# SyncE's queue in the source's order, result stores on GpSimd's queue, first row blocks modulated by feature block (adaLN block on one Trainium2 core)

## The chip, the cores and the metric

The kernel runs on one core of a Trainium2 chip. A core has TensorE (PE in the profile: matrix products and transposes; its weight loads are listed as PEld), VectorE (DVE), ScalarE (ACT), GpSimd (POOL) and SyncE (SP). SyncE computes nothing: its queue issues DMA transfers between the memory outside (DRAM) and the core's on-chip memory. ScalarE's and GpSimd's queues can issue transfers too. Each engine works through its own instructions in their order; semaphores hold an instruction until what it needs is there. The metric is the device time of one execution in microseconds.

## The reference

One adaptive-layer-norm block over x of shape (1, 2048, 576), all in float32:

```python
mod = (_silu(c) @ w_mod).reshape(c.shape[0], 6, 1, -1)
sa, ca, ga, sb, cb, gb = (mod[:, n] for n in range(6))
h = _layernorm(x, axis=-1) * (1 + ca) + sa
x = x + ga * _A_ref(h, A_wqkv, A_wo)
h = _layernorm(x, axis=-1) * (1 + cb) + sb
x = x + gb * _B_ref(h, B_w1, B_w2, B_w3, B_w4)
```

`_A_ref` is attention with 32 heads of 18 features, causal, in a sliding window of 256 positions. `_B_ref` first mixes tokens (layer norm, product with w1, gelu, four quarters of the features shifted by +1, -1, +2 and -2 positions, product with w2, added to its input) and then channels (layer norm, product with w3 to 4608 features, gelu, product with w4, added).

## The kernel before, in words

The 2048 rows are 16 row blocks of 128. The 576 features are four feature blocks of 128 and a tail of 64. Products that need float32 precision are made from parts: an operand is rounded to the matrix format (the high part), the difference is kept as a second operand (the low part), and three products (high with high, high with low, low with high) are added in PSUM, the memory that TensorE writes to.

Three phases follow one another.

**Phase A** (`phase_a`, to about 712 us) makes the modulation, the projections and the attention. `consts` makes masks on GpSimd; `vones` sets the constant columns of the 16 V tiles on GpSimd; `cond` loads c and makes silu(c), which a transpose turns into a column per feature block. `mod_load` loads the ten pieces of the modulation matrix for sa and ca (tiles wmL), `mod_mm` multiplies them with silu(c) (L243), `mod_ev` evicts the result with four activations (L250) and `mod_tr` transposes it into columns (modT, L258). `ln(t)` loads a row block (L268), makes its statistics (L85 to L89: VectorE's batch-norm instructions, then two small GpSimd instructions for the reciprocal root), normalizes it (L277), transposes it (L286, L288), and then, with the modulation as per-partition scale and shift, evicts it by feature block (L292), rounds it to the high part (L295) and subtracts for the low part on GpSimd (L297). Four row blocks share a tile hT. `vraw` and `vload` load and split the weights of V, `qload` those of q and k (L332 and the two loads L77 and L78 of `load_dup`); `vproj` (L357) projects V for a row block, `qproj` (L371) q and k for four of them, which ScalarE stores to DRAM (qkh, qkl: L376).

The attention works in 32 units: c counts four groups of 8 heads, g four groups of 512 positions, hq the two halves of a head group. A unit has a buffer of four (tiles U), made by `ualloc` (two memsets on GpSimd, L385 and L386). `uload` (L400) brings its queries and keys from DRAM in twelve DMAs. `s2` makes scores (L426) for the row maxima (L433 on VectorE), turns them into a row (L447, evicted as ms by ScalarE, L449) and writes them into the unit's queries by two DMAs on SP (L451: "the maxima"). `s3` makes the transposed scores (L476, with the mask by L477), the exponentials on ScalarE (L483, tiles P), the product with V (L498), its eviction (L503), a transpose (L510), the division on VectorE (L516, tile o), and stores o for two units at once to DRAM on SP (od, L518).

Beside the attention, `modvec` makes the other four modulation vectors: loads on SP (L189), multiplications on GpSimd (L193 to L196), a product with ones, and a store on SP (modd, L205). `woload` loads Wo, scales it with ga on GpSimd (L558), rounds it on ScalarE (L559) and subtracts on GpSimd (L560). `s4` makes the output projection of a row block: loads of od and x (L657, L659), transposes, products (L677) with the addition to x (L678) and a store (xp, L680); statistics; `ln1` modulates (L99, L101) and stores (hbd, L691); statistics again; `ln2` normalizes (L780) and stores (xnd, L696). `load_w1` and `load_w2` load and split the weights of phase B through two raw buffers (L716 to L761); the last step of `load_w2` writes the low parts of a tail into place by DMAs on SP (L761). Row blocks 12 to 15 go through `s4` in phase B.

**Phase B** (`phase_b`, to about 900 us) mixes tokens; its first row blocks are loaded from xnd (L797). **Phase C** (to the end) is the channel mix: 18 groups of 256 hidden features, products L1012 and L1041.

What sets the order: `phase_a` gives every step a time (`ev`, a list of time and function), with one attention unit as the unit of time; T0 is the time of the first projection, `shift` that of the first unit. `play` runs the steps in order of time, which writes the instructions down in that order: the source's order. Under `manual_schedule` the named engines keep this order, TensorE and GpSimd before the change. All other queues, SP among them, get their order from a planner that estimates durations and moves an instruction forward when it thinks that it could go. In phases B and C every queue is planned so.

Of the kernel before, what the change touches and what calls it, by code (L numbers as in the profile page):

```python
# [50 lines left out]
class Kern:  # L51
# [75 lines left out]
    def phase_a(self):  # L127
# [11 lines left out]
        with ExitStack() as st:  # L139
# [9 lines left out]
            ones = wp.tile([P, P], F32, name="ones")  # L149
            units = []  # L150
# [15 lines left out]
            def cond():  # L166
# [6 lines left out]
                nc.scalar.activation(sr, cr, AF.Exp, scale=-1.0)  # L173
                nc.vector.tensor_scalar(sr, sr, 1.0, None, op0=ALU.add)
# [6 lines left out]
            def modvec(v):  # L181
                acc = []
                steps = []

                def chunk(k):
                    def f():
                        w = row(f"wm{v}_{k}")
                        kk = P if k < KC else TAIL
                        nc.sync.dma_start(w[:kk], self.w_mod[k * P:k * P + kk, v * D:(v + 1) * D])  # L189
                        if k == 0:  # L190
                            acc.append(w)
                        if k == 0:
                            nc.gpsimd.tensor_scalar(w, w, silu[:, 0:1], 0.0, op0=ALU.mult, op1=ALU.add)  # L193
                        else:
                            nc.gpsimd.tensor_scalar(w[:kk], w[:kk], silu[:kk, k:k + 1], 0.0, op0=ALU.mult, op1=ALU.add)
                            nc.gpsimd.tensor_tensor(out=acc[0][:kk], in0=acc[0][:kk], in1=w[:kk], op=ALU.add)  # L196
                    return f

                def spill():
# [5 lines left out]
                    nc.sync.dma_start(self.modd[v], acc[0][0:1, :])  # L205

                steps = [chunk(k) for k in range(KC + 1)]
                return steps + [spill]
# [20 lines left out]
            def mod_bc():  # L229
                fm["s"] = fm["x"][:, 4 * P:4 * P + 32 * (KC + 1)].rearrange("p (k n) -> p k n", n=32)  # L230
                nc.vector.memset(fm["x"][:, 256:320], 0.0)
                nc.vector.tensor_copy(fm["s"], silu.unsqueeze(2).to_broadcast([P, KC + 1, 32]))

            halves = (slice(0, 256), slice(256, D))
# [11 lines left out]
            def mod_ev():  # L246
                fm["r"] = fm["x"][:, 0:320]
                for q in range(4):
                    n = halves[q % 2].stop - halves[q % 2].start
                    nc.scalar.activation(fm["r"][32 * q:32 * q + 32, 0:n], fm["p"][32 * q:32 * q + 32, 0:n], AF.Copy, bias=float(q // 2))  # L250
# [49 lines left out]

            Wv, Wq, wbuf = {}, {}, []
# [22 lines left out]

            def qload(m):
                def f():
                    raw = pp.tile([P, KC + 1, P], F32, tag="wr", name=f"rwq{m}", bufs=2)
# [3 lines left out]
                    cols = slice(m * P, (m + 1) * P)  # L331
                    nc.sync.dma_start(raw[:, 0:KC, :], self.wqkv[0:KC * P, cols].rearrange("(k p) c -> p k c", p=P))  # L332
                    self.load_dup(raw[:, KC, :], self.wqkv[KC * P:, cols])
# [13 lines left out]
            def vproj(t, z):  # L347
                def f():
                    L = hT[t // 4]
                    ts = slice((t % 4) * P, (t % 4 + 1) * P)  # L350
                    pv = dense([P, 288], f"pv{t}_{z}")
                    pl = []
                    for k in range(KC):
                        pl += [(L[:, k, ts], Wv[z, k][:, 0, :]), (L[:, k, ts], Wv[z, k][:, 1, :]), (L[:, KC + k, ts], Wv[z, k][:, 0, :])]
                    pl += [(L[:, 2 * KC, ts], Wv[z, KC][:, 0, :]), (L[:, 2 * KC, ts], Wv[z, KC][:, 1, :])]
                    for n, (a, b) in enumerate(pl):
                        nc.tensor.matmul(pv, a, b, start=(n == 0), stop=(n == len(pl) - 1))  # L357
# [21 lines left out]
            def ualloc(n):  # L379
                def f():  # L380
# [3 lines left out]
                    k = u[:, 2048:].rearrange("p (j n) -> p j n", j=2)  # L384
                    nc.gpsimd.memset(q.bitcast(F32), 0.0)  # L385
                    nc.gpsimd.memset(k.bitcast(F32), 1.0)  # L386
# [68 lines left out]
            def s3(c, g, hq):  # L455
# [50 lines left out]
                def fin2():  # L506
# [9 lines left out]
                    nc.vector.tensor_tensor(out=o[:, :, hq * 72:hq * 72 + 72].rearrange("p t (h d) -> p t h d", d=DH), in0=pt[:, :, :, 0:DH], in1=rc.unsqueeze(3).to_broadcast([P, 4, 4, DH]), op=ALU.mult)  # L516
                    if hq == 1:
                        nc.sync.dma_start(self.od[g].rearrange("(t p) d -> p t d", p=P)[:, :, c * 144:(c + 1) * 144], o)  # L518
# [10 lines left out]
                return steps, n, fin1, fin2  # L529
# [3 lines left out]
            def woload():  # L533
                steps = []

# [11 lines left out]
                steps.append(begin)  # L547

                def one(k):
                    def f():  # L550
                        raw = row(f"wor{k}")
                        if k < KC:
                            nc.sync.dma_start(raw, self.wo[k * P:(k + 1) * P, :])
                            h, l = Wo["m"][:, k, :], Wo["m"][:, KC + k, :]
                        else:
                            self.load_dup(raw, self.wo[KC * P:, :])
                            h, l = Wo["h"], Wo["l"]
                        nc.gpsimd.tensor_tensor(out=raw, in0=raw, in1=Wo["ga"], op=ALU.mult)  # L558
                        nc.scalar.copy(h, raw)  # L559
                        nc.gpsimd.tensor_tensor(out=l, in0=raw, in1=h.bitcast(F32), op=ALU.subtract)  # L560
                    return f
                return steps + [one(k) for k in range(KC + 1)]
# [8 lines left out]
            def sub3(c, g, hq, tb):  # L571
                st, n, f1, f2 = s3(c, g, hq)
                e = max(t for t, _ in st) / n * self.ww
                return [(tb + self.ww * t / n, f) for t, f in st] + [(tb + e + self.l_f, f1), (tb + e + self.l_f + self.l_o, f2)]
# [4 lines left out]
            ev = [(T0 - 2.0, consts), (T0 - 1.95, cond), (T0 - 1.97, warm(0)), (T0 - 1.9, vones), (T0 - 1.9, mod_bc)]  # L579
            for k in range(KC + 1):  # L580
                ev += [(T0 - 1.9 + 0.1 * k, mod_load(k)), (T0 - 1.3 + 0.1 * k, mod_mm(k))]
            ev += [(T0 - 0.85, mod_ev), (T0 - 0.8, mod_tr)]
# [14 lines left out]
            for kind, a, b in jobs:  # L597
# [5 lines left out]
                if kind == "v":  # L603
                    ev.append((T, vproj(a, b)))
# [5 lines left out]
            for t in range(NT):  # L610
                g, i = divmod(t, 4)
                ld, stt, nm, tr = ln(t)
                te = first["h", g] - 0.05 - (0.15 if g == 0 else 0.25) * (3 - i)
                tl = max(te - 1.6, T0 - 1.94 + 0.001 * t if t < 2 else T0 - 1.34 + 0.05 * t)
                ev += [(tl, ld), (max(te - 0.6, tl + 0.1), stt), (max(te - 0.4, tl + 0.15), nm), (te, tr)]
            ev += [(T0 - 1.35, vraw(0)), (last["v", 0] - 0.5, vraw(1))]
            for k in range(KC + 1):
                ev += [(T0 - 0.75 + 0.02 * k, vload(0, k)), (last["v", 0] + 0.01 + 0.005 * k, vload(1, k))]
            for n, m in enumerate(order):
                t1 = first["q", m] - (0.45 if m in early else 0.75)  # L620
                ev.append((t1 if n < 3 else max(t1, last["q", order[n - 3]] + 0.01), qload(m)))
            for n in range(4):
                ev.append((self.t_end - (8.99 - 3 * n) * dq, ualloc(n)))
# [3 lines left out]
            for c in range(NCH):  # L627
                for g in range(NGA):
                    for hq in range(2):
                        tb = 2 * u + hq + shift  # L630
                        ev.append((tb - self.u_ld, uload(c, g, hq)))
# [7 lines left out]
            uw = 2 * (3 * NGA) + 0.6 + shift  # L639
            ev += spread(woload(), uw, uw + 1.5)  # L640
            for n, v in enumerate((2, 3, 4, 5)):
                mv = modvec(v)
                ev += spread(mv[:-1], shift + 8.0 + 2.5 * n, shift + 10.0 + 2.5 * n)
                ev.append((shift + 11.3 + 2.5 * n, mv[-1]))
            ev += spread(self.load_w1(), 2 * u - 2 + 1.9 + shift, 2 * u + 1.6 + shift)
            ev += spread(self.load_w2(), 2 * u + 1.6 + shift, 2 * u + 2.4 + shift)
            with self.tc.manual_schedule(engines={mybir.EngineType.PE, mybir.EngineType.Pool}):
                play(ev)

    def s4(self, g, i):  # L650
# [14 lines left out]
        def wo(hf):  # L665
            def f():
# [12 lines left out]
                if hf == 1:  # L679
                    nc.sync.dma_start(self.xp[t], x)  # L680
# [7 lines left out]
        def ln1():  # L688
            x = box["x"]
            self.modulate(x, x, *box["s"], self.cb, self.sb, self.m_s4)  # L690
            nc.sync.dma_start(self.hbd[t], x)  # L691
# [421 lines left out]
```

## Time and profile before

| | |
|---|---|
| median of 3 runs | 1824.18 us (lowest 1822.40, one run of 5885.22) |
| the profiled execution | 1823.32 us |
| its span, first to last instruction | 1821.2 us |
| TensorE busy | 1744.1 us |
| VectorE, ScalarE, GpSimd busy | 979.7, 605.8, 386.1 us |
| mean granted TensorE clock | 0.982 |
| moved by DMA | 156.88 MB, 136.09 of them issued by SP |

Times in the profile are in us from the span's start. A row of a timeline gives start, duration, engine, line, operation, output and inputs by name, form and count, and in brackets the idle time before it and what ended that time. In the lists of waits a row reads: engine, tile and line that waited, what it waited for, then the total in us, how often, and the longest. SPq is SP's queue of DMA issues. U is a unit's buffer, wmL the modulation weights, wor and Wom are Wo raw and split, xr is a row block in `s4`, xn one in phase B.

### The profile page before, as it was taken

The page shows a single profiled execution, that of the slowest core. Times are in us where ns is not written, and L with a number is a line of the kernel's source. Part 1 is how long each engine was busy: PE and PEld are TensorE (multiplying, and loading weights), DVE is VectorE, ACT ScalarE, POOL GpSimd, SP SyncE. Part 2 cuts the span into 40 slices and gives each one's busy share as a digit, 9 for nine tenths or more (in the row PEclk, how much of TensorE's full clock was granted, in tenths as well). Part 3 has the DMA queues.
Part 4 walks back from the last instruction along what each step waited for, and adds up shares of the span by engine and source line. Part 5 has one row for each costly group of instructions (what it writes and reads, how often), then busy time and mean ns, then how long its engine had stood idle before and what let it go on. Part 6 is the DMA issues. An engine that isn't in the chain of part 4 may idle for free.

```text
span 1821.2 us, 30288 instructions
## 1 busy us (share of the span) xinstructions
PE 1744.1 (96%) x11700; PEld 1503.8 (83%) x11700; DVE 979.7 (54%) x2670; ACT 605.8 (33%) x1292; POOL 386.1 (21%) x376
## 2 busy tenths in 40 slices
PE   7999889989988998999899999999999999999999
PEld 5898666666665776999899999999999999999998
DVE  5302377767766887787744444444444444444434
ACT  5722156556555444444321111211111121111111
POOL 4511220022002111111313332333322111111100
PEclk8999999999999999999999999999999999999999
DMA  6424433454334455642301111111101000000002
GB/s 206 128 95 146 172 108 95 116 130 117 104 110 136 159 182 177 227 133 71 103 28 54 40 54 35 48 54 54 41 29 35 22 20 28 28 28 28 1 1 104
DMA packets 97904, 156.88 MB, mean 86 GB/s; under 512 B 11226, under 2 KB 40670, under 8 KB 97762
## 3 DMA queue, kind: packets, MB, share of 16 engines
q1 hardware_dynamic: 87394, 136.09, 25.3%
q10 hardware_dynamic: 10368, 18.88, 2.8%
q8 instruction: 92, 1.51, 0.3%
q14 instruction: 50, 0.41, 0.1%
HBM read 107.06 MB, written 47.20 MB: 85 GB/s over the span
## 4 chain that ended last, share of the span: by engine, by line
PE 56%; DVE 2%; POOL 0%; DMA 0%; issue 0%; ACT 0%; SPq 0%; POOLq 0%; ACTq 0%; DVEq 0%
PE p L1041 25%; PE p L1012 21%; PE pg L853 2%; PE w L906 2%; PE p L1014 2%; PE p L1013 2%; DVE x L907 0%; PE po L677 0%; DVE xr L99 0%; DMA r<-in_B_w_dram 0%; DVE G L871 0%; POOL CW L996 0%; DVE xm L780 0%; DVE LNT L70 0%; DVE G L858 0%
## 5 line engine op out<-in xcount | busy, mean ns | idle before, releaser
L1041 PEld LDWEIGHTS p<-CW,Gc 128*128 128x128 f32 x3456 | 474.4, 188 | 16.2 <-DVE Gc L1023 3.7
L1041 PE MATMUL p<-CW,Gc 128*128 128x288 f32 x3456 | 482.8, 295 | 3.4 <-DVE Gc L1023 3.4
L1012 PE MATMUL p<-LNT,CW 128*128 128x512 f32 x1728 | 419.8, 391 | 0.0
L1012 PEld LDWEIGHTS p<-LNT,CW 128*128 128x128 f32 x1728 | 316.7, 188 | 58.9
L1020 ACT ACTIVATE gfc<-p 128x512 f32<-128x512 f32 x144 | 86.1, 598 | 735.5 <-PE p L1014 735.5
L433 DVE CUSTOM_DVE_ANT_0 sc<-sc,mask 128x384 f32<-128x384 f32 (+2 forms) x512 | 262.9, 552 | 119.8 <-PE sc L426 116.9
L1045 DVE TENSOR_TENSOR acc<-p,acc 128x288 f32<-128x288 f32 x340 | 152.9, 454 | 316.1 <-PE p L1041 312.7
L483 ACT ACTIVATE P<-X 128x384 f32<-128x384 f32 x480 | 223.9, 489 | 148.6 <-PE X L477 143.4
L426 PE MATMUL sc<-U 126*128 126x384 f32 (+2 forms) x512 | 205.5, 415 | 29.8 <-DMA U<-qkl 13.9
L476 PE MATMUL X<-U 128*128 128x384 f32 (+2 forms) x704 | 182.6, 317 | 8.2 <-ACT P L483 7.6
L476 PEld LDWEIGHTS X<-U 128*128 128x128 f32 x704 | 128.7, 194 | 37.9 <-issue 26.1
L1045 DVE TENSOR_TENSOR accw<-p,accw 128x288 f32<-128x288 f32 x204 | 89.8, 452 | 130.1 <-PE p L1041 128.4
L477 PE MATMUL X<-maskb,identb 128*128 128x256 bf16 x480 | 138.3, 288 | 0.0
L426 PEld LDWEIGHTS sc<-U 126*128 126x128 f32 x512 | 101.3, 203 | 42.7 <-DVE m L433 17.5
L1023 DVE TENSOR_TENSOR Gc<-gfc,Gc 128x512 fp32r<-128x512 f32 x144 | 129.0, 896 | 4.7
L371 PE MATMUL pq<-hT,Wq 128*128 128x512 f32 x504 | 122.1, 401 | 0.7 <-DVE m L433 0.7
L371 PEld LDWEIGHTS pq<-hT,Wq 128*128 128x128 f32 x504 | 95.2, 191 | 23.3 <-DVE m L433 1.1
L992 POOL TENSOR_TENSOR CW<-r,CW 128x1024 fp32r<-128x1024 f32 x17 | 41.3, 2427 | 280.6 <-DVE CW L990 280.6
L498 PE MATMUL av<-P,V 128*32 128x256 f32 (+2 forms) x1472 | 96.6, 391 | 0.7 <-ACT P L483 0.7
L1022 ACT CAST Gc<-gfc 128x512 fp32r<-128x512 f32 x144 | 89.5, 621 | 4.6
L996 POOL TENSOR_TENSOR CW<-r,CW 128x1152 fp32r<-128x1152 f32 x17 | 46.4, 2727 | 158.5 <-DVE CW L995 158.5
L477 PEld LDWEIGHTS <-identb 128*128 128x128 bf16 x480 | 46.7, 97 | 38.7 <-issue 22.8
(1075 smaller groups left out, 1967.2 us busy)
## 6 DMA issues: line engine op xcount, KB each, us to landing
U<-qkh SPq DMA_DIRECT2D x160, 72.0 KB
U<-qkh SPq DMA_DIRECT2D x96, 108.0 KB
r<-in_B_w_dram SPq DMA_DIRECT2D x18, 576.0 KB
qkh<-hl ACTq DMA_DIRECT2D x36, 256.0 KB
qkl<-hl ACTq DMA_DIRECT2D x36, 256.0 KB
r<-in_B_w_dram SPq DMA_DIRECT2D x18, 512.0 KB
U<-qkl SPq DMA_DIRECT2D x80, 72.0 KB
U<-qkl SPq DMA_DIRECT2D x48, 108.0 KB
```

The costliest lines, as they stand in the source:

```text
L371: nc.tensor.matmul(pq, a, b, start=(n == 0), stop=(n == len(pl) - 1))
L426: nc.tensor.matmul(sc[:, lo:], QZ[:KR, q, i * P:(i + 1) * P], KZ[:KR, j, i * P + lo:(i + 3) * P], start=True, stop=True)
L433: nc.vector.tensor_tensor_reduce(out=sc[:, lo:], in0=sc[:, lo:], in1=mask[:, lo:], scale=1.0, scalar=-3e38, op0=ALU.add, op1=ALU.max, accu ...
L476: nc.tensor.matmul(X[:, x0:x0 + nb, :].rearrange("p a b -> p (a b)"), KZ[:, j, kb * P:(kb + 1) * P], QZ[:, q, qb * P:(qb + nb) * P], start ...
L477: nc.tensor.matmul(X[:, 0::2, :], self.identb, mk, start=False, stop=True)
L483: nc.scalar.activation(Pb[b][:, q, :], Xb[b, q].rearrange("p a b -> p (a b)"), AF.Exp, scale=SCALE)
L498: nc.tensor.matmul(abox[0][32 * q:32 * q + 32, q0:q0 + w], V[4 * g + kb][:, hv:hv + 32], Pb[b][:, q, p0:p0 + w], start=(first and n == 0), ...
L1012: nc.tensor.matmul(pg, W3[:, ws, fs], L[:, xs, :], start=(i == 0), stop=False)
L1022: nc.scalar.copy(Gh, gf)
L1023: nc.vector.tensor_tensor(out=Gl, in0=gf, in1=Gh.bitcast(F32), op=ALU.subtract)
L1041: nc.tensor.matmul(po, a, w, start=(i == 0), stop=(i == len(seq) - 1))
L1045: nc.vector.tensor_tensor(out=acc[t][:, cs], in0=po, in1=acc[t][:, cs], op=ALU.add)
```

## The change

SP joins the engines that keep the source's order, and the source is rearranged for it. Loads become steps of their own with times ahead of their use (`qdma`, `load`, `get`, the first part of `woload`). On SP there remain loads, the maxima (L451), the eight small writes of L761 and, for row blocks 12 to 15, the three stores of `s4`. The stores of the attention output, of the modulation vectors and of `s4` for row blocks 0 to 11 become steps of their own on GpSimd's queue, shortly after the step that makes their data. `uload` moves from 0.5 to 0.8 of a unit ahead of its unit, though not ahead of its buffer's memset; that puts it right behind the maxima of the unit two before. `ualloc` clears keys before queries. Wo's rounding moves from ScalarE to GpSimd, and its loads start 1.2 units earlier. `cond` is cut in two; `vones` moves behind the first row blocks.

The first four row blocks no longer go through `tr`. Their loads and the raw weights of V stand ahead of the modulation weights on SP. They are normalized and transposed while those load, into one PSUM tile per feature block for all four row blocks (`tr0`, `tr0b`). When the modulation is there, `ev0` makes per feature block one activation of 128x512 that writes the high part, the same product and sum on VectorE in float32, and the subtraction (GpSimd for three of the four, VectorE for one). Their V projections are cut into three passes over the four row blocks: high parts, tail, low parts. `mod_ev` becomes one activation with a bias column.

The diff, cut:

```diff
+    manual = {mybir.EngineType.PE, mybir.EngineType.Pool, mybir.EngineType.SP}
...
-    u0, u_ld = -1.55, 0.5
+    u0, u_ld = -1.55, 0.8
...
-    l_n, l_x, l_nb, g_s4 = 0.0, 0.3, 0.1, 0.7
+    l_n, l_x, l_nb, g_s4 = 0.05, 0.3, 0.1, 0.7
+    l_s, l_p = 0.1, 0.02
...
+            def tr0b(i):
+                def f():
+                    x, cs = xrows[i], slice(i * P, (i + 1) * P)
+                    for k in range(KC):
+                        nc.tensor.transpose(fm["pa"][k][:, cs], x[:, k * P:(k + 1) * P], self.ident)
+                    nc.tensor.transpose(fm["pb"][:, cs], x[:, KC * P:D], self.ident)
+                return f
+
+            def ev0():
+                L, pa, pb = hT[0], fm["pa"], fm["pb"]
+                r = slice(0, P)
+                for k in range(KC):
+                    nc.scalar.activation(L[:, k, :], pa[k], AF.Identity, bias=mod_col(0, k, r), scale=mod_col(1, k, r))
+                    h = xrows[k][:, 0:512]
+                    nc.vector.tensor_scalar(h, pa[k], mod_col(1, k, r), mod_col(0, k, r), op0=ALU.mult, op1=ALU.add)
+                    (nc.gpsimd if k < 3 else nc.vector).tensor_tensor(out=L[:, KC + k, :], in0=h, in1=L[:, k, :].bitcast(F32), op=ALU.subtract)
...
+                nc.scalar.activation(fm["r"], fm["p"], AF.Identity, bias=vone)
...
+                    p0 = [(L[:, k, ts], Wv[z, k][:, n, :]) for k in range(KC) for n in range(2)]
+                    p1 = [(L[:, 2 * KC, ts], Wv[z, KC][:, 0, :]), (L[:, 2 * KC, ts], Wv[z, KC][:, 1, :])]
+                    p2 = [(L[:, KC + k, ts], Wv[z, k][:, 0, :]) for k in range(KC)]
...
+                    nc.gpsimd.memset(k.bitcast(F32), 1.0)
                     nc.gpsimd.memset(q.bitcast(F32), 0.0)
-                    nc.gpsimd.memset(k.bitcast(F32), 1.0)
...
+                def fin3():
                     if hq == 1:
-                        nc.sync.dma_start(self.od[g].rearrange("(t p) d -> p t d", p=P)[:, :, c * 144:(c + 1) * 144], o)
+                        nc.gpsimd.dma_start(self.od[g].rearrange("(t p) d -> p t d", p=P)[:, :, c * 144:(c + 1) * 144], orow[c, g])
...
+                def store():
+                    nc.gpsimd.dma_start(self.modd[v], acc[0][0:1, :])
...
-                        nc.scalar.copy(h, raw)
+                        nc.gpsimd.tensor_copy(h, raws[k])
...
+                        n = 2 * u + hq
+                        tu = tb - self.u_ld
+                        ev.append((max(tu, ta[n] + 0.01) if n < 4 else tu, uload(c, g, hq)))
...
-            uw = 2 * (3 * NGA) + 0.6 + shift
+            uw = 2 * (3 * NGA) - 0.6 + shift
...
-                if hf == 1:
-                    nc.sync.dma_start(self.xp[t], x)
...
+        def put(d):
+            def f():
+                (nc.gpsimd if g < 3 else nc.sync).dma_start(d[t], box["x"])
             return f
...
+        return list(zip(d, (load, tr, wo(0), wo(1)))) + [(d[3] + self.l_p, put(self.xp)), (d[4], stat("b")), (d[4] + self.l_n, ln1), (d[4] + self.l_n + self.l_p, put(self.hbd)), (d[5], stat("c")), (d[5] + self.l_n, ln2), (d[5] + self.l_n + self.l_p, put(self.xnd))]
```

201 lines of the change are left out of this document (132 added, 69 removed).

## The prediction

> **What bounds the kernel now.** First the head of the page, then busy time cut at the borders of the stages (columns: stretch, length, busy time of PE, its weight loads, VectorE (DVE), ScalarE (ACT), GpSimd (POOL), then the granted TensorE clock and DMA).
>
> ```profile
> span 1821.2 us, 30288 instructions
> ...
> PE 1744.1 (96%) x11700; PEld 1503.8 (83%) x11700; DVE 979.7 (54%) x2670; ACT 605.8 (33%) x1292; POOL 386.1 (21%) x376
> ```
> ```profile
> 0.00:26.50 26.50, 16.37 (x81) 7.58 (x81) 12.68 (x37) 11.29 (x30) 10.15 (x58) 0.74 0.71 211
> ...
> 200.00:250.00 50.00, 41.32 (x222) 30.42 (x224) 27.02 (x103) 13.12 (x26) 15.79 (x14) 0.90 0.41 130
> ...
> 340.00:530.00 190.00, 174.47 (x1540) 124.66 (x1538) 136.46 (x520) 112.12 (x242) 28.01 (x27) 0.97 0.43 113
> 530.00:570.00 40.00, 33.06 (x259) 21.41 (x261) 21.95 (x87) 21.24 (x45) 13.92 (x10) 0.87 0.54 144
> 570.00:712.00 142.00, 130.67 (x1080) 103.28 (x1072) 115.83 (x361) 69.08 (x166) 16.96 (x42) 0.99 0.54 169
> ...
> 900.00:1821.00 921.00, 914.05 (x5446) 831.86 (x5444) 402.14 (x775) 174.71 (x288) 217.89 (x115) 1.00 0.12 38
> ```
>
> Half of the span (900 to 1821) is TensorE at full clock with 7 us of idle time, and the change does not touch its code. Over the whole kernel TensorE idles 77 us (1821 - 1744). What can be won lies in four places where it waits and where the granted clock then drops: the start, the first attention units (200 to 250), the units up to 570, and the border at 712 to 724. I price each by its own rows.
>
> **The start, first row blocks.** The timeline of all engines:
>
> ```profile
> 2.24 5.43 SPq L226 DMA_DIRECT2D wmL<-in_w_mod_dram  x10
> ...
> 15.23 0.74 PE L243 MATMUL pm<-wmL,modx 64*32 64x256 f32 x8 [0.83 <-DMA wmL<-in_w_mod_dram]
> 16.03 1.64 ACT L250 ACTIVATE modx<-pm 32x256 f32<-32x256 f32 x4 [10.63 <-PE pm L243]
> ...
> 19.04 1.09 PE L286 MATMUL hT0pa<-ident,x 128*128 128x128 f32 x4 [0.41 <-DVE modT L259]
> ...
> 23.82 2.71 POOL L297 TENSOR_TENSOR hT<-x,hT 128x512 fp32r<-128x512 f32 x2
> ...
> 26.50 7.25 PE L357 MATMUL pv<-Wv,hT 128*128 128x288 f32 x42
> ```
> ```profile
> L1020 ACT ACTIVATE gfc<-p 128x512 f32<-128x512 f32 x144 | 86.1, 598 | 735.5 <-PE p L1014 735.5
> ```
>
> The last modulation weight lands just before 15.23, the vector is ready at 19.04, and the first projection starts 7.5 us later, because transposes, four narrow activations and a cast per row block come after the vector. Added: the transposes run while the weights load, four wide activations (one per feature block) write the high part directly, at 0.6 us each by the 598 ns row; VectorE repeats them (taken as the same 0.6), and the low parts cost GpSimd 1.3 us each (half of 2.71) for three of the four. The projections are cut in three, so the high parts of all four row blocks run while the low ones are made. Removed: three of four evictions of 0.41 us (1.64/4), so 1.2 us. So the vector is ready 2.6 us after the last weight instead of 3.8, and the first projection starts 0.8 us after it; its first row block is paced by the four activations, 2.4 us, against about 1 at matmul rate: 1.5 lost. Without a later landing the gain would be 1.2 + (7.5 - 0.8) - 1.5 = 6.4 us.
>
> But two row blocks and the value weights, 2 x 288 + 720 KB = 1.33 MB, now stand ahead of the modulation weights. The floor is issue time, five DMAs at 0.54 us (5.43/10), 2.7 us; the ceiling is 6.3 us, the bytes at the stage's 211 GB/s. I take 3.4, nearer the floor, because the queue already held other loads when these landed. **Gain 3 us, bounds 0 to 3.7.** The ones for V move behind this work on GpSimd; they are needed only when the first projection is copied out, and 58 instructions in 10.15 us leave room.
>
> **The first attention units.** SP's issues, then TensorE:
>
> ```profile
> 200.96 0.64 SPq L400 DMA_DIRECT2D U<-qkl  x2
> ...
> 233.65 1.37 SPq L400 DMA_DIRECT2D U<-qkh  x4
> ```
> ```profile
> 203.38 1.33 PE L426 MATMUL sc<-U 126*128 126x128 f32 x4 [2.95 <-DMA U<-qkl]
> ...
> 237.08 0.41 PE L426 MATMUL sc<-U 126*128 126x384 f32 x1 [1.66 <-DMA U<-qkh]
> ```
>
> A load lands about 2.4 us after its issue (200.96 to 203.38). Two waits of this kind hold TensorE, and the clock is 0.90 over these 50 us, 5 us of lost clock. The change clears the key part of a buffer first and loads keys first, in that order, and all twelve loads of a unit follow at once behind the maxima of the unit two before. The stage idles 8.7 us. The loads can still wait for ScalarE's big stores of q and k, which stay. Bounds: nothing to 8.7 + 5 = 13.7; I take **4 us**, both waits shortened by half with half of the clock that they cost.
>
> **The steady units.** Who TensorE waits for from 250 to 530 (total, times, longest), the same for SP, and one unit's issues on SP:
>
> ```profile
> PE sc L426 <- DMA U<-qkl: 9.4, 14, 1.8
> PE sc L426 <- DVE mr L440: 2.6, 3, 1.2
> ...
> PE sc L426 <- DMA U<-qkh: 1.8, 2, 1.2
> PE sc L426 <- DMA od<-o: 1.1, 1, 1.1
> ```
> ```profile
> SPq L518 <- DVE o L516: 21.8, 11, 2.9
> ```
> ```profile
> 280.07 1.21 SPq L451 DMA_DIRECT2D U<-ms  x2
> ...
> 286.98 0.39 SPq L518 DMA_DIRECT2D od<-o  x1
> ```
>
> At 17 unit starts (14 + 2 + 1) the loads came last: 9.4 + 1.8 + 1.1 = 12.3 us. SP stood 21.8 us in front of the stores of the attention output, waiting for VectorE, with the rest of a unit's loads queued behind. The stores go to GpSimd, whose work here is 28 us in 190; behind a waiting store there stand only multiplications of modulation rows, and they have a unit's time. What is late next: where loads were in time, VectorE held three starts for 0.9 us each (2.6/3). If that took the place everywhere the gain were 0; if nowhere, 12.3, and with the clock of 340 to 530 (0.03 x 190 = 5.7) 18. I take two thirds of 12.3 and a third of 5.7: **10 us**.
>
> The Trainium skill (DMA: Bandwidth & Descriptors, section "Issuing engines are not separate DMA queues") says that spreading DMAs over engines saves only sequencer time. By that the store's own 0.39 us is all that moves and the gain here would be nothing; the 21.8 us row says that it is the wait in front that counts, which that section does not discuss.
>
> **Wo.** Waits of ScalarE, then of TensorE, 530 to 570:
>
> ```profile
> ACT Wom L559 <- POOL wor L558: 7.6, 4, 2.9
> ...
> ACT Woh L559 <- POOL wor L558: 1.7, 1, 1.7
> ```
> ```profile
> PE X L476 <- ACT P L483: 6.0, 4, 2.9
> ```
>
> ScalarE stands 9.3 us in front of five casts that wait for GpSimd, with the exponentials behind them; TensorE loses 6.0 us, and 0.13 x 40 = 5.2 us of clock. The casts move to GpSimd, where they cost between 0.6 (the 128x512 activation, the nearest single-input row) and 1.4 us (half of 2.71, two inputs); five of either fit into its idle 26 us of 40. **Gain 6.0 plus half of 5.2, 8.5 us; bounds 5 to 11.**
>
> **The blocks after attention (570 to 712) and the border.** VectorE is busy 116 of 142 us here. Three stores per block and 12 blocks go to GpSimd, between the reciprocal roots that it makes for the same blocks:
>
> ```profile
> 606.38 0.82 DVE L101 SCALAR_TENSOR_TENSOR xr<-xr,b0rs,sb 128x576 f32<-128x576 f32 x1
> ...
> 608.33 0.19 DVE L87 BATCH_NORM_AGGREGATE c0mv<-c0st 128x2 f32<-128x12 f32 x1
> ...
> 610.23 0.57 DVE L780 TENSOR_SCALAR xr<-xr,c0mv,c0rs 128x576 f32<-128x576 f32 x1
> ```
> ```profile
> 608.62 0.22 POOL L88 TENSOR_SCALAR c0rs<-c0mv 128x1 f32<-128x1 f32 x1 [8.05 <-DVE c0mv L87]
> 608.92 0.57 POOL L89 TENSOR_TENSOR c0rs<-c0rs,mhalf 128x1 f32<-128x1 f32 x1
> ```
>
> The store of the modulated row may start at 607.2 and the root is wanted at 608.6: 1.4 us of cover, and 0.7 more until VectorE asks (609.5 to 610.2), of which I count 0.4. No row shows a store issued from GpSimd: at SP's 0.39 or at GpSimd's own 1.4 for a tile of this size it is hidden. I cost it at **0**, bounds +4 (SP free of its waits) and, if a store holds GpSimd longer, the slower rival below.
>
> The Trainium skill (SBUF — State Buffer, section "A bandwidth-pool intuition that's wrong (but worth ruling out)") gives a GpSimd-issued DMA 0.62 us alone and 3.1 beside a VectorE copy in a two-port mode. By 3.1 the sum would be 12 x 1.3 = 16 us worse, 1813, an estimate from that page; the 0.57 us for 576 elements at 610.23 is no faster than an element per ns, which does not look like such a mode.
>
> At the border SP issues the last weights and then phase B's first rows:
>
> ```profile
> 719.31 2.46 SPq L761 DMA_DIRECT2D W2t<-rw2l  x4
> ...
> 730.49 2.42 SPq L761 DMA_DIRECT2D W2t<-rw2l  x4
> ...
> 733.62 0.87 SPq L797 DMA_DIRECT2D xn<-xnd  x2
> ```
> ```profile
> 722.13 1.09 PE L951 MATMUL xnT1pa<-ident,xn 128*128 128x128 f32 x4 [4.77 <-DMA xn<-xnd]
> ```
>
> Now row blocks 0 and 1 are loaded ahead of these weights. Whether they may still pass in the new order I can't tell: 0, bounds +5 and -14 (below).
>
> **Sum.** 3 + 4 + 10 + 8.5 = 25.5 us, rounded to 26. The profiled execution took 1823.3 us, span 1821.2 and 2.1 around it (the median of the runs shown is 1824.2): **1797 us**, 1.4% faster. About 2% (36.5 us) is what a measurement of this kernel tells from no change.
>
> **Rivals.**
> - *Everything is recovered* (0.22). The waits vanish and the clock with them: 3.7 + 9 + 16 + 11 = 40 us, 1783. For it: unit starts with no wait at all occur now. Against: VectorE's waits stand close behind.
> - *The loads stay late* (0.13). Twelve issues at 0.34 (1.37/4) and 2.4 to land are 6.5 us, with the maxima in front 7.7. The source gives them 0.85 of a unit, 10.8 us of 12.7 (280 us for 22 units, two to each of the 11 stores): a late maximum or a short unit uses that up. Then the first units and the steady ones give nothing: 1823 - 3 - 8.5 = 1811. This is what the DMA page's rule comes to.
> - *The border gets worse* (0.10). If SP keeps the source's order, blocks 0 and 1 are issued after 733 and land at 736 instead of 722: 14 us, 1811.
> - *Stores on GpSimd delay the roots* (0.10), the slower case. Each of 12 blocks loses d - 1.8 us for a store that holds GpSimd for d; from d = 4.0 the 26 us are gone; at d = 5 it is 12 x 3.2 = 38 us: 1835.
>
> **Numbers.** Forecast 0.45. Range 1778 to 1822: from beyond the full recovery to just under today's time, leaving out the store case and some of the lower tail; the likeliest case alone is 1787 to 1806. Faster by over 2% (below 1787): 0.22 and a little of the forecast's tail, 0.25; slower by over 2% needs d beyond 7 us: 0.03; the rest 0.72.
>
> **What would show it.** Right: first projection near 22 us; SP's waits for VectorE's attention output gone, "PE sc <- DMA U" from 250 to 530 below 5 us; no wait of ScalarE in front of Wo; phase C as long as before. Wrong: unit starts still waiting for U; VectorE waiting for GpSimd's roots between 570 and 712; a gap over 10 us before the first transposes of phase B; the time saved early given back there.

## The result, and the profile after

The changed kernel takes 1897.55 us (median of 4 runs, 1895.92 to 1901.5) where the kernel before takes 1827.27 beside it: a ratio of 1.0397, 95% interval 1.036 to 1.0434. (One of the four runs behind the 1827.27 took 5885.22 us; the ratio leaves it out.) The prediction said 1797 and a range up to 1822; it has the wrong sign. The head of the page after:

```profile
span 1894.1 us, 30311 instructions
...
PE 1769.1 (93%) x11700; PEld 1522.6 (80%) x11700; DVE 987.2 (52%) x2673; ACT 597.2 (32%) x1262; POOL 427.1 (23%) x436
```

The span grew by 72.9 us and TensorE's busy time by 25 (1769.1 - 1744.1) with the same 11700 instructions: it waits 48 us more, and its own work takes longer at a lower clock. The stages, in the columns of the prediction's table:

```profile
0.00:22.00 22.00, 13.49 (x80) 6.99 (x80) 10.52 (x36) 4.61 (x10) 6.31 (x23) 0.92 0.88 251
...
250.00:340.00 90.00, 77.52 (x643) 54.72 (x641) 56.31 (x214) 48.98 (x105) 9.69 (x10) 0.92 0.34 93
340.00:530.00 190.00, 157.96 (x1299) 111.52 (x1301) 118.82 (x451) 94.90 (x204) 37.05 (x39) 0.92 0.40 102
530.00:600.00 70.00, 61.26 (x523) 42.66 (x515) 40.87 (x160) 36.89 (x81) 15.68 (x15) 0.90 0.38 103
600.00:775.00 175.00, 145.95 (x1158) 115.69 (x1158) 123.85 (x390) 74.13 (x174) 39.95 (x73) 0.94 0.46 142
...
973.00:1894.00 921.00, 913.44 (x5450) 831.18 (x5448) 402.90 (x776) 174.77 (x289) 217.70 (x116) 1.00 0.12 38
```

Phase C is untouched (921 us in both). From 340 to 530 TensorE did 1299 instructions where it did 1540, at a clock of 0.92 instead of 0.97.

A ruler for all runs is the store of the maxima, one per unit (the first of the two DMAs that write ms into U on the timeline): how far apart these stores lie over the first 27 units, how long the last four take (they run beside the blocks behind the attention), and what comes behind the last. Before, the first stood at 226.00, the 28th at 587.20, the last at 681.97; after, at 223.56, 637.93 and 750.43. So the 72.9 us are: -2.4 at the start; 27 units at 15.35 us instead of 13.38, +53.2; the last four in 112.5 us instead of 94.8, +17.7; behind them 1143.7 us instead of 1139.2, +4.4. All figures by this ruler come from one profiled execution of each kernel.

**The steady units.** What TensorE waits for from 250 to 600, and then SP:

```profile
PE sc L477 <- DMA U<-qkl: 33.1, 29, 3.9
PE sc L477 <- DMA U<-qkh: 10.3, 7, 2.1
```
```profile
SPq L502 <- ACT P L534: 185.7, 22, 10.8
```

SP now stands 185.7 us in 22 units in front of the store of the maxima (L502, L451 in the kernel before), and 36 waits of TensorE (29 + 7), 43.4 us, are for loads of U. (The row names ScalarE's exponentials; what SP needs is the copy ms, L500, which ScalarE makes between them.) One turn on the timeline of all engines:

```profile
332.94 1.22 SPq L502 DMA_DIRECT2D U<-ms  x2
334.26 0.42 SPq L451 DMA_DIRECT2D U<-qkl  x1
...
338.36 0.32 SPq L451 DMA_DIRECT2D U<-qkl  x1
...
341.26 0.30 PE L477 MATMUL sc<-U 126*128 126x128 f32 x1 [0.27 <-DMA U<-qkl]
...
344.44 0.48 PE L498 MATMUL mT<-identr,mr 128*8 128x128 f32 x4
345.11 0.56 ACT L500 CAST ms<-mT 8x512 fp32r<-8x512 f32 x1
345.69 1.23 SPq L502 DMA_DIRECT2D U<-ms  x2
347.02 0.41 SPq L451 DMA_DIRECT2D U<-qkl  x1
...
351.96 0.61 SPq L451 DMA_DIRECT2D U<-qkl  x1
352.67 2.11 SPq L196 DMA_DIRECT2D wm<-in_w_mod_dram  x2
...
358.50 0.41 PE L477 MATMUL sc<-U 126*128 126x384 f32 x1 [3.86 <-DMA U<-qkl]
```

Read it as a ring: a unit starts at 341.26 when its loads have landed; the transposes of the maxima of the unit before (L498) stand 3.2 us behind this start in TensorE's order; only then can ScalarE copy and SP store them (345.69); only behind that store does SP issue the twelve loads of the next unit; these land at 358.50. 4.4 us from start to store and 12.8 from store to next start are 17.2, and the unit's own work is less than 12 (11.8 a unit in u_early, below). From 354.8 to the next store, at 361.7, SP issues nothing. In the kernel before the planner moved some of a unit's loads, here four of twelve, past the store:

```profile
313.08 0.36 SPq L400 DMA_DIRECT2D U<-qkl  x1
313.49 1.13 SPq L400 DMA_DIRECT2D U<-qkh  x3
317.35 1.22 SPq L451 DMA_DIRECT2D U<-ms  x2
318.61 0.46 SPq L400 DMA_DIRECT2D U<-qkh  x1
```

### The profile page after: what moved, and what is told of

Read it like the earlier page. It is cut to its first block, busy times and chain, and to the rows that moved or that the text cites. A ratio compares the mean times of both kernels' runs of the same rounds, so it can differ in the third digit from the quotient of the medians.

```text
span 1894.1 us, 30311 instructions
## 1 busy us (share of the span) xinstructions
PE 1769.1 (93%) x11700; PEld 1522.6 (80%) x11700; DVE 987.2 (52%) x2673; ACT 597.2 (32%) x1262; POOL 427.1 (23%) x436
## 3 DMA queue, kind: packets, MB, share of 16 engines
q0 software_dynamic: 4288, 15.35, 2.3%
## 4 chain that ended last, share of the span: by engine, by line
PE 74%; DMA 15%; DVE 5%; SPq 1%; POOL 1%; issue 1%; ACT 1%; ACTq 0%; DVEq 0%; POOLq 0%
PE p L1148 24%; PE p L1119 20%; DMA U<-qkl 7%; PE pq L422 5%; DMA U<-qkh 5%; PE av L549 3%; PE po L764 3%; PE pg L960 3%; PE sc L477 3%; PE pv L406 3%; PE X L527 3%; PE w L1013 2%; PE p L1121 2%; PE p L1120 2%; PE X L528 1%
## 5 line engine op out<-in xcount | busy, mean ns | idle before, releaser
L477 PE MATMUL sc<-U 126*128 126x384 f32 (+2 forms) x512 | 211.6, 427 | 72.1 <-DMA U<-qkl 41.4
L527 PE MATMUL X<-U 128*128 128x384 f32 (+2 forms) x704 | 189.3, 327 | 11.3 <-DVE oT L74 8.2
L477 PEld LDWEIGHTS sc<-U 126*128 126x128 f32 x512 | 106.1, 213 | 87.2 <-issue 48.3
L527 PEld LDWEIGHTS X<-U 128*128 128x128 f32 x704 | 133.9, 202 | 41.1 <-issue 25.2
L528 PE MATMUL X<-maskb,identb 128*128 128x256 bf16 x480 | 142.9, 298 | 0.0
L549 PE MATMUL av<-P,V 128*32 128x256 f32 (+2 forms) x1472 | 101.9, 415 | 0.0
```

Of the source, the lines that this page charges most:

```text
L477: nc.tensor.matmul(sc[:, lo:], QZ[:KR, q, i * P:(i + 1) * P], KZ[:KR, j, i * P + lo:(i + 3) * P], start=True, stop=True)
L527: nc.tensor.matmul(X[:, x0:x0 + nb, :].rearrange("p a b -> p (a b)"), KZ[:, j, kb * P:(kb + 1) * P], QZ[:, q, qb * P:(qb + nb) * P], start ...
L528: nc.tensor.matmul(X[:, 0::2, :], self.identb, mk, start=False, stop=True)
L549: nc.tensor.matmul(abox[0][32 * q:32 * q + 32, q0:q0 + w], V[4 * g + kb][:, hv:hv + 32], Pb[b][:, q, p0:p0 + w], start=(first and n == 0), ...
```

## The experiments

Times are medians; ratios are to the kernel before run beside it, with 95% intervals. (The kernel before took 1821.8 to 1827.9 beside the several runs, so between rows it is the ratios that compare.) "Unit" is the mean interval between maxima stores over the first 27, "last 4" the four behind, in us from the profile.

| run | time | ratio | unit | last 4 |
|---|---|---|---|---|
| before (its profile) | 1823.3 | | 13.38 | 94.8 |
| changed | 1897.6 | 1.0397 [1.036, 1.0434] | 15.35 | 112.5 |
| u_early | 1805.2 | 0.9905 [0.9879, 0.993] | 11.82 | 107.1 |
| sp_planned | 1831.4 | 1.0046 [1.0025, 1.0067] | 12.90 | 114.9 |
| max_act | 1831.6 | 1.0043 [1.0027, 1.0058] | 12.10 | 123.5 |
| od_sp | 1895.7 | 1.0408 [1.0377, 1.0438] | 15.32 | 116.4 |
| u4 | 1806.1 | 0.9923 [0.9897, 0.9948] | 12.16 | 107.8 |
| u4_lp | 1818.4 | 0.998 [0.9964, 0.9995] | 12.12 | 114.6 |
| u4_puts_act | 1809.6 | 0.9937 [0.9917, 0.9956] | 12.13 | 112.4 |
| planned_puts_sp | 1806.6 | 0.9905 [0.9876, 0.9934] | 13.02 | 92.1 |
| planned_pool | 1851.5 | 1.0136 [1.0105, 1.0167] | 12.43 | 129.5 |
| planned_xp_sp | 1823.5 | 0.9997 [0.9981, 1.0013] | 12.85 | 104.5 |
| planned_xp_pool | 1829.4 | 1.0036 [1.0015, 1.0057] | 12.89 | 113.9 |
| start_only | 1823.3 | 1.0000 [0.9979, 1.0021] | 13.24 | 93.9 |
| before_u | 1811.7 | 0.9936 [0.9911, 0.996] | 12.73 | 98.2 |
| u4_wo_act | 1814.9 | 0.994 [0.9918, 0.9962] | 12.63 | 107.6 |
| hybrid | 1788.1 | 0.9782 [0.9754, 0.9809] | 12.18 | 95.0 |
| hybrid_ma | 1776.7 | 0.9727 [0.9709, 0.9744] | 11.83 | 96.1 |

### Is it the place of the loads, or the stores on GpSimd?

**u_early**, one number of the changed kernel:

```diff
-    u0, u_ld = -1.55, 0.8
+    u0, u_ld = -1.55, 1.2
```

> The changed kernel with one number changed: the twelve loads of an attention unit come 1.2 units ahead of its scores in SyncE's written order, not 0.8, so ahead of the maxima store of the unit two before it and not behind it. Theory A (the loop: maxima store, then twelve loads, then landing, then the next scores, whose first matmuls stand ahead of the next maxima): the interval from one maxima store to the next over the first 27 units, 15.35 us in the changed kernel (223.56 to 637.93), falls to between 12.4 and 13.6, TensorE's waits for U between 250 and 600 us fall from 43 us to under 10, and the time is 1835 to 1855, since the last four units (112.5 us, 94.8 before) have another cause. Theory B (the stores on GpSimd's queue are at fault, by their share of the DMA engines or by holding GpSimd): the order of SyncE is not the point, the interval stays over 14.8 and the time at 1885 or more.

Some 90 us come back (92 by the medians), more than the 42 to 62 that theory A said, and theory B is out: the stores are still on GpSimd. The maxima of unit n are stored at n + 1.15 in the written order, the loads of unit n + 2 stood at n + 1.2. At n + 0.8 they stand behind the maxima of the unit before, so each load has a whole unit more; any value from 0.85 to 1.85 gives the same order of the two. TensorE from 250 to 600 no longer waits for them at the scores:

```profile
PE sc L477 <- DVE m L484: 5.1, 1, 5.1
PE oTT0pa L68 <- DMA or<-od: 3.5, 1, 3.5
PE X L527 <- DMA U<-qkl: 2.0, 1, 2.0
PE X L527 <- DMA U<-ms: 1.5, 1, 1.5
```

**sp_planned**: `manual` loses SP, so that the planner orders it.

> The changed kernel with SyncE's order given back to the planner; TensorE's and GpSimd's stay written out, the stores stay on GpSimd and the first row blocks as changed. Theory A: the interval between maxima stores goes back to 13.4 us or below and the last four units to 95 us; what is left are the gains at the start (about 3 us) and at Wo, so 1810 to 1828. Theory B: 1885 or more, since GpSimd keeps the stores.

The units come back (12.90, better than before's 13.38), the last four don't: 114.9, not 95. So the loss has two parts, and the second one is there without SP's written order too.

**max_act**: the two stores of L502 go out on `nc.scalar` instead of `nc.sync`.

> The changed kernel with the two maxima stores of each unit issued by ScalarE right behind the copy that they read, so that SyncE is left with loads alone and nothing stands between a freed U buffer and its loads but their place in the order. ScalarE pays two issues a unit (about 0.6 us each by SyncE's row of 1.22 us for two). Theory A: interval 12.4 to 13.6 us over the first 27 units, time 1835 to 1860. Theory B: interval over 14.8, 1885 or more, and ScalarE's issues add up to 20 us to that.

12.10 a unit: loads that stand behind nothing that waits for a result are in time, by another way than u_early's. The last four grow to 123.5; why is not shown.

**od_sp**: the stores of L571 back on `nc.sync`.

> The changed kernel with the store of the attention rows (od, 16 of them, 288 KB each) back on SyncE at its written place. Theory B: the time falls to 1830 to 1860. Theory A: no gain; SyncE now also stands in front of these stores, which come out 0.1 unit behind the rows, at about 2.7 units behind the unit's start, so between 1890 and 1925.

No change: in the changed kernel, where the ring sets the pace, the stores of the attention rows cost the units nothing on either queue.

### The first units

**u4**: units 0 to 3 keep 0.8, the rest 1.2.

```diff
-                        tu = tb - self.u_ld
+                        tu = tb - (self.u_ld if n < 4 else 1.2)
```

> The run with loads 1.2 units ahead, except that units 0 to 3 keep 0.8. In that run the first maxima store came at 231.30 us, 7.7 behind the changed kernel's 223.56, and TensorE waited 7.0 us once for it: SyncE stood in front of the loads of units 2 and 3, whose buffers the projections still held. If that is the cause, the first maxima store is back at 224 us, the interval over 27 units stays at 11.8 to 12.1 and the time is 1796 to 1800. If the projections' own transfers are the cause, nothing changes: 1803 to 1807.

The first store is back at 223.61, but the next intervals are 16.6 and 14.8 us where u_early had 11.7 and 10.4: the wait only moved to the next units, and the span is the same (1804.6 and 1804.4). The expectation missed.

**before_u**: the same 1.2 from unit 4 on in the kernel before.

> The kernel before with the loads of the units from 4 on at 1.2 units ahead of the scores, not 0.5; nothing else. If the place of the loads in the written order is what counts, also where the planner may move them: 12.0 to 12.6 us a unit in place of 13.38, so 20 to 35 us less. If the planner places the loads by its own measure of what is urgent: within 5 us of the kernel before.

0.65 us less a unit, 12 us in all: the written place counts under the planner too, by less than was expected. SP's wait for od, then TensorE's at the scores, in this run from 250 to 530:

```profile
SPq L518 <- DVE o L516: 41.8, 11, 4.9
```
```profile
PE sc L426 <- DMA U<-qkl: 1.2, 1, 1.2
```

SP stood twice as long in front of the od stores as before (21.8), and yet TensorE's waits for U at the scores fell from 11.2 us in 16 to this one. (Behind them, at the transposed scores, 12.0 us in nine are new, 7.9 of them for the maxima.)

### The last four units

**planned_puts_sp**: sp_planned, and `put` always on `nc.sync`.

> The run with SyncE planned (last four units 114.9 us, 1829.9) with the stores of the twelve blocks back on SyncE's planned queue, as the kernel before had them; the od and modulation stores stay on GpSimd. Theory C: last four units back to 95 to 98, time 1808 to 1814. Theory D is silent on this (SyncE is planned in both), and if the last four units stay over 110, neither holds and it is the other edits of that stage (the casts, the W1 and W2 loads, the order of the events).

92.1 us instead of 114.9: the 36 stores of the blocks on GpSimd cost 22.8 us there. Two runs ask whether it is their place in GpSimd's order:

**u4_lp**: u4 with `l_p` 0.25 in place of 0.02; **u4_puts_act**: u4 with the stores on `nc.scalar`.

> The run before with one more number changed: in the blocks behind the attention (12 of 16) a store comes 0.25 units behind the step that makes its row in GpSimd's written order, not 0.02, so that a store that waits for VectorE no longer stands right ahead of the root of the block before it. Theory C (GpSimd's stores hold the roots, VectorE stands for the roots and the scores' maxima behind it, TensorE for these): the last four units, 107.1 us against 94.8 in the kernel before, fall to 93 to 99 and the time falls by 8 to 14. Theory D (SyncE's written order of the blocks' loads is at fault): the last four units stay within 3 us of 107.

> The run u4 with the 36 stores of those twelve blocks issued by ScalarE and not by GpSimd. Theory C: last four units 93 to 99 us, time down by 8 to 14 us, less what ScalarE's issues (36 of 0.35 to 0.6 us) cost the exponentials behind them. Theory D: no change but for these.

Neither helps; later stores make it worse (114.6). SP's written order by itself doesn't show as the cause either: with the stores on GpSimd the last four take 114.9 with SP planned and 107 to 113 with its order written (u_early, u4, the changed kernel). Giving GpSimd's order to the planner doesn't help either:

**planned_pool**: `manual` holds TensorE alone.

> The changed kernel with GpSimd's order, as well as SyncE's, given back to the planner; all stores stay on GpSimd's queue. The last four units took 114.9 us with GpSimd's order written out and SyncE planned, and 92.1 with the stores of the blocks on SyncE. Theory C (it is the written order: a store that waits for VectorE stands ahead of a root that is ready): 92 to 99 us, time 1806 to 1815. Theory E (it is the store itself: issued by GpSimd it comes later and takes longer, and the next step overwrites its row in place): over 105 us, 1820 or more.

129.5 us, as theory E said, and not better. (The first maxima store of this run comes 12 us late, at 237.87, which is part of its time.)

**planned_xp_sp** and **planned_xp_pool**: sp_planned with only xp on `nc.sync`, or only xp on GpSimd.

> The run with SyncE planned (last four units 114.9 us) with one of the three stores of a block, that of the row behind Wo (xp), back on SyncE; hbd and xnd stay on GpSimd. In that run GpSimd stood 58.6 us in front of xp stores and 18.3 in front of the other two. Theory C (a store at which GpSimd stands holds the root behind it): nearly all comes back, 92 to 98 us. Theory E (each store is late by itself and the row is overwritten in place): a third comes back, 104 to 110.

> The other way round: xp alone on GpSimd, hbd and xnd on SyncE. Theory C: 108 to 116 us for the last four units. Theory E: 96 to 102.

The first speaks for theory E (104.5), the second for C (113.9): each alone fits one run only, so both seem to happen. xp alone on GpSimd costs 21.8 us (113.9 - 92.1), the other two alone 12.4 (104.5 - 92.1), all three 22.8: the costs overlap and don't add. In sp_planned (timeline) the root of block 1 stands behind the store of block 2:

```profile
614.59 0.19 DVE L87 BATCH_NORM_AGGREGATE c1mv<-c1st 128x2 f32<-128x12 f32 x1
...
618.31 0.54 POOL L770 DMA_DIRECT2D xp<-xr  x1 [4.64 <-DVE xr L765]
618.88 0.24 POOL L88 TENSOR_SCALAR c1rs<-c1mv 128x1 f32<-128x1 f32 x1
...
619.80 0.58 DVE L887 TENSOR_SCALAR xr<-xr,c1mv,c1rs 128x576 f32<-128x576 f32 x1 [0.26 <-POOL c1rs L89]
...
620.78 0.82 DVE L99 SCALAR_TENSOR_TENSOR xr<-xr,b2mv,cb 128x576 f32<-128x576 f32 x1 [0.28 <-DMA xp<-xr]
621.51 0.68 DVE L70 TENSOR_TENSOR oT<-oTT3pa,oT 128x512 fp32r<-128x512 f32 x1
...
622.57 0.45 PE L527 MATMUL X<-U 128*128 128x256 f32 x2 [2.03 <-DVE oT L74]
```

The variance is there at 614.8, the root starts 4.1 us later, because GpSimd stands in front of the xp store; VectorE stands only 0.26 us for the root itself, but in its own order the copies of oT (L70) come behind the step that needs the root (L887) and behind one that waits for the xp store (L99), and TensorE waits 2.03 us for these copies. In planned_puts_sp the root follows at once, and the copies of oT come ahead of that step (612.21 and 613.42):

```profile
607.11 0.19 DVE L87 BATCH_NORM_AGGREGATE c1mv<-c1st 128x2 f32<-128x12 f32 x1
607.39 0.22 POOL L88 TENSOR_SCALAR c1rs<-c1mv 128x1 f32<-128x1 f32 x1 [5.89 <-DVE c1mv L87]
```

In planned_pool the root follows at once too, and VectorE stands for the store itself, because the next step overwrites the row in place:

```profile
615.16 0.22 POOL L88 TENSOR_SCALAR c1rs<-c1mv 128x1 f32<-128x1 f32 x1 [1.20 <-DVE c1mv L87]
...
621.15 0.58 DVE L887 TENSOR_SCALAR xr<-xr,c1mv,c1rs 128x576 f32<-128x576 f32 x1 [6.09 <-DMA hbd<-xr]
```

Such waits for hbd come to 18.2 us in 6 from 587 to 710 in planned_pool, and 12.6 in 5 from 587 to 700 in planned_xp_sp. Over the whole table, all runs with the 36 stores on SP take 92 to 98 us for the last four, all others 104 to 130. But SP is planned there in all runs of the first kind; none keeps SP's written order and has these stores on SP. So for the changed kernel itself it stays open how far each mechanism goes, and what SP's order adds.

### Single terms

**start_only**: the edits of the start in the kernel before, nothing else.

> The kernel before with the edits of the start alone: the first row blocks modulated by feature block, the earlier loads and the split weight loads of the projections; attention, Wo, the blocks behind it and SyncE's planning as before. By the prediction's terms: 3 us at the start and 4 in the first units, so 7 us below the kernel before, with bounds 0 and 17. If the planner gives the start back in the first units, as in the run with SyncE planned (first maxima store 225.69 against 226.00): within 2 us of the kernel before.

No gain that can be told: the interval reaches 3.8 us to either side, and the 7 us of the prediction's terms lie outside it. The first projection comes at 22.50 in this run, 4 us earlier, the first maxima store 1.1 us earlier (224.88).

**u4_wo_act**: `nc.gpsimd.tensor_copy(h, raws[k])` becomes `nc.scalar.copy(h, raws[k])`.

> The run u4 with the five rounding copies of Wo back on ScalarE. By the term of the prediction (8.5 us, bounds 5 to 11) the time rises by 5 to 11 us over u4, all of it between the 22nd and the 27th maxima store. If ScalarE's copies were hidden, or ScalarE only took them late because its own order in the kernel before was another, the time stays within 3 us of u4.

ScalarE's wait is back (its waits from 490 to 560),

```profile
ACT Wom L618 <- POOL wor L612: 8.4, 3, 3.8
```

and the two units there take 16.89 and 18.92 us, not 12.45 and 13.77: 9.6 us, in the predicted bounds. The ratios differ by only 0.0017, 3 us, with overlapping intervals; as a time of the whole it is unclear.

### Together

**hybrid**: u4 up to unit 27.3; behind it SP planned, with the blocks' stores on SP. **hybrid_ma**: all loads at 1.2, and the maxima of the first four units on ScalarE.

```diff
             with self.tc.manual_schedule(engines=self.manual):
-                play(ev)
+                ev = play(ev, 2 * u - 4.7 + shift)
+            with self.tc.manual_schedule(engines=self.manual - {mybir.EngineType.SP}):
+                play(ev)
...
-                (nc.gpsimd if g < 3 else nc.sync).dma_start(d[t], box["x"])
+                nc.sync.dma_start(d[t], box["x"])
...
-                        nc.sync.dma_start(QZ[KR + n:KR + n + 1, :, :].bitcast(F32), ms[4 * n:4 * n + 4, :].bitcast(F32))
+                        (nc.scalar if c == 0 and g < 2 else nc.sync).dma_start(QZ[KR + n:KR + n + 1, :, :].bitcast(F32), ms[4 * n:4 * n + 4, :].bitcast(F32))
```

> The run u4 (loads 1.2 units ahead from unit 4 on, SyncE's order written out) up to 27.3 units, and from there SyncE planned again with the blocks' stores on its queue, as in the run with 92.1 us in the last four units. If the two causes are independent: 12.1 to 12.2 us a unit over the first 27, 92 to 97 for the last four, 1138 to 1145 behind the last maxima store, so 1782 to 1794. If the planner's late part depends on how the early part was laid out: over 1798.

> The run hybrid with all units' loads 1.2 ahead and the maxima stores of the first four units issued by ScalarE, so that no store stands behind loads whose buffers the projections still hold. The first four intervals, 16.6, 14.8, 12.4 and 11.9 us in u4, become 11 to 12.5 each, as in the run with all maxima on ScalarE, the rest stays: 5 to 9 us below hybrid, 1775 to 1787. If only SyncE's issue in the projections counts, no gain over hybrid.

hybrid came as expected, hybrid_ma 11 us below it, a little more than expected (its first intervals are 11.1, 10.6, 12.4 and 12.6). hybrid_ma is 2.7% faster than the kernel before and the fastest here; its page and its stage from 250 to 500:

```profile
span 1776.7 us, 30246 instructions
...
PE 1726.6 (97%) x11700; PEld 1499.8 (84%) x11700; DVE 976.9 (55%) x2673; ACT 594.5 (33%) x1262; POOL 406.8 (23%) x400
```
```profile
250.00:500.00 250.00, 244.98 (x2285) 178.87 (x2284) 198.00 (x764) 167.47 (x363) 52.55 (x55) 1.00 0.49 133
```

TensorE is busy 98% of that stage, at full clock.

## Why the prediction was wrong

**The step that failed: the steady units** ("10 us", bounds 0 to 18; measured -53.2 over the first 27 units, in which the first units and Wo lie too). It took SP's 21.8 us in front of the od stores for what made loads late. before_u speaks against it: that wait doubled, and nearly all loads were in time. (The kernel before with the od stores alone moved was not run.) The larger row of the same answer (250 to 530, before) was passed over:

```profile
SPq L451 <- ACT P L483: 102.6, 22, 7.4
```

SP stood nearly five times as long in front of the store of the maxima; it stays on SP, and the change puts all twelve loads behind it. u_early and max_act, which take the loads out from behind it in two ways, bring 11.82 and 12.10 us a unit.

The rival "the loads stay late" named the place and mis-sized three things. The cover of 10.8 us (0.85 unit) was counted from the written time of the store; in the run the store leaves 4.4 us behind the next unit's start, because TensorE and ScalarE reach it late, which leaves 8.3 of 12.7. The need of 7.7 us took the issues back to back and 2.4 us to land; it measured 8.3 (332.94 to 341.26) in one turn and 12.8 in the next, where two loads of wm and an od store were issued beside them. And the price was "no gain", 1811, as if a late load cost only what the loads before had cost; but store and next start wait for each other in a ring, every unit pays, and the clock falls to 0.92 with it. Store and issues took 5.4 and 6.3 us of the 8.3 and 12.8, up to the last load (332.94 to 338.36, 345.69 to 351.96); the rest, 2.9 and 6.5, is the landing. So within the 7.7 it was mainly the landing, put at 2.4, that was too small; what made it slower in the second turn, no run shows by itself.

**The blocks behind the attention** (0, bounds +4, and the rival "stores on GpSimd delay the roots", d = 5, 1835): the rival's place and sign were right, its mechanism half. An issue holds GpSimd for d = 0.54 to 0.65 us, so the price by d was nothing; GpSimd stands in front of a store whose row isn't ready, 12.5 us before one xp store in the changed kernel, and the term has no such wait. The last four units took 17.7 us more; with SP planned the stores on GpSimd account for 22.8, and the split in the changed kernel stays open.

**The start** (3, bounds 0 to 3.7): 2.4 us at the first maxima store.

```profile
21.28 2.79 ACT L330 ACTIVATE hT<-hT0p,modT 128x512 fp32r<-128x512 f32 x4 [0.84 <-DVE modT L270]
...
22.11 10.89 PE L406 MATMUL pv<-Wv,hT 128*128 128x288 f32 x56 [1.07 <-ACT hT L330]
...
35.73 3.30 PE L422 MATMUL pq<-hT,Wq 128*128 128x512 f32 x13 [1.41 <-POOL Wq L380]
```

The first projection comes at 22.11, "near 22" as said, 0.8 behind the vector. The 56 products behind it take 10.89 us, at 7.25 for 42 before they would take 9.7, and the next group waits 1.4 for a weight that GpSimd splits late. The prediction set 1.5 us for the slower first projections; they lost 1.2 and the wait. In start_only 1.1 us are left at the first maxima store, and no gain in the time can be told.

**The first units** (4, bounds 0 to 13.7): TensorE waits 7.7 us in three for U from 185 to 250, before it waited 5.8 in three; the second maxima store comes 0.6 us earlier than before (240.67, 241.27). The same ring has begun; the term is gone.

**Wo** (8.5, bounds 5 to 11): right where the loads are in time. ScalarE no longer waits in front of Wo, and in u4 putting its copies back costs 9.6 us there.

**The border** (0, bounds -14 to +5 in time gained): 4.4 us worse behind the last maxima store, inside the bounds. The wait of 4.77 us for the first rows of phase B is gone.

Two slips in its sums changed little: one of the 17 waits counted as late loads names the od store, and *Everything is recovered* puts 9 and 16 us where the upper bounds are 13.7 and 18, without a reason.

The Trainium skill's rule (DMA: Bandwidth & Descriptors, "Issuing engines are not separate DMA queues"), that another issuing engine saves only sequencer time, holds for the od stores: od_sp, 1.0408 against 1.0397. It doesn't cover stores that wait in front of other work: there the choice of the queue was worth 22.8 us. The Trainium skill's 3.1 us for a GpSimd-issued DMA beside VectorE (SBUF — State Buffer, "A bandwidth-pool intuition that's wrong (but worth ruling out)") did not show as time for which an issue holds GpSimd: 0.54 to 0.99 us for each of the 52 stores of 288 KB in the changed kernel.

## What to carry to other kernels

On a queue that keeps a written order, list what each entry waits for; if the loads of the next turn stand behind a store that can only go once this turn has begun, store and loads close a ring, and its length, not the engines' work, sets the pace. Look for the longest wait on that queue in the profile, not for the one that the change removes. A store moved to an engine that also makes small results can hold these back until its row is ready, and a next step that overwrites the row in place waits for the store.

## What the runs showed of the hardware

An issue of a 288 KB store takes 0.54 to 0.65 us on GpSimd for contiguous rows and 0.75 to 0.99 for the attention rows (the changed kernel); on SP the medians of the kernel before are 0.32 to 0.34 and 0.39 us. Stores of 288 KB from GpSimd landed 3.0 to 3.9 us behind their issue in the changed kernel (medians by kind of store); single ones held their row longer, as the 7.8 us of hbd in planned_pool (613.33 to 621.15). An issue of the 8 KB maxima takes the same median of 0.58 us from ScalarE (max_act) as from SP.
